# Casting loads in batch 0 for seven GpSimd casts, and VectorE's list of batch 0 in another order

## The chip, the cores and the metric

The kernel runs on one core of a Trainium2 chip. Time is device microseconds of that core for one execution, the median of several runs; lower is better. Five engines run lists of their own and wait for each other through semaphores: TensorE (PE, matmuls, with weight loads as PEld beside them), VectorE (DVE), ScalarE (ACT), GpSimd (POOL) and SyncE (SP). DMAs are issued from SP's and POOL's lists. A list is run strictly in order: an instruction that waits holds everything behind it on its engine.

## The reference

Two parts in a row, for eight batches of S = 3072 tokens with D = 256, a query width of 64 and a hidden width of 1024:

```python
scores = (1.0 / S) * np.matmul(z, z.transpose(0, 2, 1))
attn = np.maximum(scores, 0.0) ** 2
x = u * np.matmul(attn, v)
h1 = x @ w1
h2 = x @ w2
g = np.maximum(h1, h2)
out = g @ w_out
```

All inputs and the output are float32; the kernel computes in bfloat16 with float32 sums.

## The kernel before

**Scores.** `z` is laid out transposed in `zT`. A batch's scores are cut into 6 x 6 blocks of 512 x 512. Scores are symmetric, so only the upper triangle is computed: `score_pair` (L248) makes half a block, that is two tiles of 128 keys by 512 queries. Two matmuls go to PSUM (`s_ps`, L267), a ReLU copies them out (L277 in one piece, L284 in two halves on ACT; L282 is a half on VectorE for pairs called "shared"), and `finish()` squares them: L294 on VectorE in one operation of 1024 columns, L290 in halves, L292 on ACT. The lower blocks are made by a transposing DMA on SP's queue (`mirror`, L315). A block lives in one of 27 homes (`Block`, taken from the list `free`); `mirror_ready` issues a mirror only while more than one home is free.

**Batch 0, groups 0 to 3** (`PLAIN` = 4, the loop from L946). A group is 512 queries. `attn_unit` (L331) multiplies 24 key tiles by both halves of `v`, two 64-row matmuls per step. Between the steps, at slots given by hand, the loop emits score pairs (at most 11 ahead of what PE needs), and at chosen tile numbers `n` all the other work: the group's sums (`drain_fast`, L355 and L356, then L982), the product with `u` (`gate`, L499), the transposes of `u` (`turn_u`, L243), loads and casts.

**Loads and casts.** `load_u` and `load_v` are DMAs from POOL's queue that cast float32 to bfloat16 on the way (L235, L209). `staged` (L164) instead loads float32 from SP's queue into a `Block`; `load_staged` (L172) and `z_staged` (L178) then cast on POOL. The homes used for staging rest in a list until `rested` gives them back. At the start, tokens 12 to 23 of `z` are loaded as float32 from POOL's queue and cast by POOL (L147).

**Weights.** max(h1, h2) is computed as ReLU(x(w1 - w2)) + x w2, and the second term needs only `W2o` = w2 w_out. So `w15` = w1 - w2 is made on VectorE (L1022), w2 is transposed on PE (L1027) and copied out (L1028), and `W2o` is a matmul of that with `w_out` (L1035).

**The first feed-forward parts.** Groups go in couples. `second(i, tasks)` runs the feed-forward of a couple and puts a list of tasks, nearly all on VectorE, ahead of it in program order: for the first two couples `ff` (L746 inner, L768 outer products, L759 ReLU), later `ff_by_seven`, which uses a seven-product form of the matrix product with four weight forms `wT_sb` (`weight_forms`, L531 to L536).

**Groups 4 and up, couple by couple** (L1239). Attention too uses seven products instead of eight, with combinations of `v` (`combine_v`, four operations per piece, L223 to L226) and of score blocks (`prepare` and `combine`, L369). Some combinations are made early, in the list ahead of the feed-forward before; others late, between the steps. A combination S3 of batch 1 is written over a block that a mirror's DMA still reads. Batch 0's last couple mixes both ways (`MIXED_LANES`). Sums leave PSUM through `kept` (L1137, a copy) and `add` (L1133).

**The order of the tasks.** `prepared(i)` returns v's combinations and the early forms, per piece of `v`: four v operations, then two forms. Just before the first `ff`, `first` is the number of tasks put ahead of it.

The lines that the change touches are the two that hold the order of gates and of weight forms,

```python
                if i and n in (12, 15):
                    tasks[n // 15]()
```

```python
            second(i - 1, tasks, **({} if b else {"order": (2, 3, 0, 1)}))
            if not b:
                for do in weight_forms():
                    do()
```

and the ones in the diff below.

Of the kernel before, what the change touches and what calls it, by code (L numbers as in the profile page):

```python
# [12 lines left out]
def kernel(  # L13
# [10 lines left out]
    nc = tc.nc  # L24
# [15 lines left out]
    NC = NG // 2  # L40
# [36 lines left out]
    def by_tile(x):  # L77
        return x.rearrange("(p t) d -> p t d", t=NT)
# [151 lines left out]

    un, uT = {}, {}

    def load_u(b, g):
        un[b, g] = unat.tile([P, G, D], bf16, name="un")
        nc.gpsimd.dma_start(out=un[b, g], in_=by_tile(u[b])[:, ds(g * G, G), :])  # L235

    def u_staged(b, g):
# [609 lines left out]
    def emit_pair(wait=0, shared=False, act=False, late=False):  # L847
        nonlocal done
        shared = shared or done < 12 and done % 3 == 0
        finish = score_pair(  # L850
            *pairs[done], dve_half=1 if shared else None, halves=done == 0, act=act
        )
        done += 1
        if late:
            late_squares.append(finish)
        elif wait:
            due.append((tick + wait, finish))
        else:
            finish()
# [33 lines left out]
    with tc.manual_schedule():  # L893
# [4 lines left out]
        nc.vector.memset(warm[:, P:], 0.0)  # L898
        load_v(0, 0, 0, G)
        make_identity(nc, ident)  # L900
        z32.update({lo: first_z(lo, n, nc.gpsimd) for lo, n in ((12, 8), (20, 4))})
        load_v(0, 0, G, G)
        for piece in range(1, NC):
            for lo in (0, G):
                load_v(0, piece, lo, G)
        load_u(0, 0)
        load_u(0, 1)
        z_first.append(Block())
        for pad in (-1, NT):
            nc.vector.memset(z_bf16(pad, 1), 0.0)  # L910
        w2, w2T = Block(), Block()
# [23 lines left out]
        keep_warm([P] * 5)  # L935
        cast_z(nc.scalar.copy, z32[5], 5, 3)
        cast_z(nc.vector.tensor_copy, z32[5], 8, 4, at=3)
        for at in range(0, 8, 4):
            cast_z(nc.gpsimd.tensor_copy, z32[12], 12 + at, 4, at=at)
        cast_z(nc.gpsimd.tensor_copy, z32[20], 20, 4)  # L940
        emit_pair()
        zT_pe(5, 7, [(nc.scalar.copy, 3), (nc.vector.tensor_copy, 4)])
        keep_warm([P] * 2)
# [5 lines left out]
        for i in range(PLAIN):  # L949
            b, g = groups[i]  # L950
            if i:
                acc = new_acc()
            if i == 3:
                rested(len(resting) - 1)
            new, slots = {}, pair_slots(i)
            for slot, (n, dc) in enumerate(steps_of(i)):
                k = need(b, g, n)
                upto = max(k, min(done + 1, k + AHEAD)) if slot in slots else k
                while done < min(upto, len(pairs)):
                    emit_pair(  # L960
                        wait=int(i < 2 and slot == slots[-1]), shared=i == 3 and done % 3 == 1
                    )
                if i == 0 and slot in (8, 22):
                    if slot == 8:
                        zT_pe(12, 8, [(nc.scalar.copy, 4)] * 2)
                    else:
                        zT_pe(20, 5, [(nc.scalar.copy, 5)])
                    if slot == 22:
                        for x in z_first:
                            x.release()  # L970
                attn_unit(b, g, n, acc, dc, n == 0, n == NT - 1)
                if n == NT - 1 and i < PLAIN - 1:
                    if i < 2:
                        new[dc] = drain_fast(acc, dc)
                        flush()
                    else:
                        new.update(drain(acc, [dc]))
                if dc:
                    continue
                if i in (1, 2) and n in (6, 9):  # L980
                    h = sums[n // 9]
                    nc.vector.tensor_add(h[0], h[0], h[1])  # L982
                    sums[n // 9] = h[0]
                if i and n == 12:
                    xTs[groups[i - 1]], tasks = gate(*groups[i - 1], sums)
                if i and n in (12, 15):
                    tasks[n // 15]()
                if i == 0 and n == 14:
                    turn_u(0, 0)
                if (i, n) == (0, 16):  # L990
                    turn_u(0, 1)
                if (i, n) == (0, 20):
                    nc.vector.memset(w2_sb[:, 0, 0:1], 0.0)
                    nc.gpsimd.dma_start(out=w2_sb, in_=by_chunk(moe_w2))
                if (i, n) == (1, 9):
                    w1_32 = [staged(w2_sb[:, c : c + 1], by_chunk(moe_w1)[:, c : c + 1]) for c in range(KD)]
                if (i, n) == (1, 11):
                    u_staged(0, 2)
                if (i, n) == (1, 13):
                    for h in range(2):  # L1000
                        part = slice(h * KF // 2, (h + 1) * KF // 2)
                        load_staged(w_out_sb[:, part], by_chunk(moe_w_out)[:, part])
                if (i, n) in ((1, 15), (2, 14), (3, 4)):
                    z_staged(1, i - 1)
                if (i, n) == (2, 2):
                    turn_u(0, 2)
                if (i, n) == (2, 5):
                    u_staged(0, 3)
                if (i, n) == (2, 17):
                    turn_u(0, 3)  # L1010
                if (i, n) in ((2, 18), (3, 1)):
                    u_staged(0, 4 + (i > 2))
                if (i, n) in ((2, 10), (3, 10)):
                    turn_z(1, i - 2)
                if (i, n) == (3, 16):
                    turn_z(1, 2)
                if later and n % 4 == 0 and (i == 3 or i and n > 12):
                    later.sort(key=lambda block: (block[2] > 3, block[1], block[2]))
                    mirror(*later.pop(0))
                if i == 2 and n == 16:  # L1020
                    for c in range(KD):
                        nc.vector.tensor_sub(w15_sb[:, c : c + 1], w1_32[c], w2_sb[:, c : c + 1])  # L1022
                if i == 2 and n in (15, 18):
                    half = n // 18
                    tp = mm_tile([P, KF, P], bf16, "tpw")[0]
                    for j in range(KF):
                        nc.tensor.transpose(tp[:, j, :], w2_sb[:, half, ts(j, P)], ident)  # L1027
                    nc.scalar.copy(w2T_sb[:, half, :, :], tp)  # L1028
                if i == 2 and n == 18:
                    w2.release()  # L1030
            if i == 2:
                for dc in range(KD):
                    ps = mm_tile([P, D], fp32, "w2o_ps")[0]
                    for nb in range(KF):
                        nc.tensor.matmul(  # L1035
                            ps,
                            w2T_sb[:, dc, nb, :],
                            w_out_sb[:, nb, :],
                            start=(nb == 0),
                            stop=(nb == KF - 1),  # L1040
                        )
                    nc.scalar.copy(W2o_sb[:, dc, :], ps)
                w2T.release()
            sums = new
# [25 lines left out]
        def prepared(i):  # L1070

            b, c = couples[i]
            for o in range(NC):
                assert all(
                    pair_at[b, min(q, k), 2 * max(q, k) + 1] < done
                    for q in (2 * c, 2 * c + 1)
                    for k in (2 * o, 2 * o + 1)
                ), (i, done)
            forms, early, late = prepare(b, c)
            split = {}  # L1080
            for n, o in enumerate(forms):
                if (b, o) not in vt:
                    split[n] = combine_v(b, o)
            if not b:
                return forms, [do for dos in split.values() for do in dos] + early, [], late
            last_v = split.pop(NC - 1, []) if b > 1 else []
            early = [
                do for n in range(NC) for do in split.get(n, []) + early[2 * n : 2 * n + 2]
            ]
            return forms, early, last_v, late  # L1090

        b, g = groups[PLAIN - 1]
# [5 lines left out]
        loads_behind(PLAIN // 2 - 1)  # L1098
        forms, early, last_v, late = prepared(PLAIN // 2)
        first = 4 * NC + len(forms)  # L1100
        second(PLAIN // 2 - 2, sums + early[:first])
        xTs[b, g], gates = gate(b, g, {dc: h[0] for dc, h in halves.items()})
        for do in gates + early[first:]:
            do()
# [2 lines left out]
        for i in range(PLAIN // 2, len(couples)):  # L1107
# [10 lines left out]
            n_pairs = target - done  # L1118
            at_step = {}
            for n in range(n_pairs):  # L1120
                at_step.setdefault(2 + n * (len(steps) - 2) // max(n_pairs, 1), []).append(n)
            acc, opened, h = {}, {}, {}
            left = {}
            if not b:
# [9 lines left out]

            def kept(name, of):
                h[name] = new_h()
                nc.scalar.copy(h[name], acc[of])  # L1137

            def after_p5():
                add(h["V"], h["V"], acc["P5"])  # L1140
# [144 lines left out]
                ]  # L1285
            mm_pool("mm_single")
            second(i - 1, tasks, **({} if b else {"order": (2, 3, 0, 1)}))
            if not b:
                for do in weight_forms():
                    do()  # L1290
            if at_last:
                for do in token_forms(b, c):
                    do()
# [38 lines left out]
```

## Time and profile before

| | |
|---|---|
| median of 3 runs | 890.31 us (889.68 to 890.57) |
| the profiled execution: its own time | 890.65 us |
| its span, first to last instruction | 888.7 us |
| granted TensorE clock | 1.00 |
| PE busy | 879.2 us, 99% |
| VectorE busy | 796.7 us, 90% |
| ACT busy | 723.2 us, 81% |
| POOL busy | 100.6 us, 11% |

Times inside a profile count from the span's start. Groups 0 to 3 of batch 0 run from about 6 to 63 us, the first feed-forward from 63 to 79, batch 0's last couple from 79 to 103, the second feed-forward from 103 to 119, and batch 1's first couple from 119 to 141. By stage (busy us of each engine):

| window us | PE | VectorE | ACT | POOL |
|---|---|---|---|---|
| 20 to 36 | 15.85 | 12.05 | 14.22 | 0.43 |
| 36 to 43 | 7.00 | 6.30 | 6.54 | 6.46 |
| 62 to 80 | 17.89 | 11.69 | 12.24 | 3.43 |
| 104 to 119 | 14.95 | 10.80 | 10.17 | 0.00 |
| 119 to 136 | 16.48 | 16.90 | 14.42 | 2.12 |

In a line of the order of time, the columns are start, duration, engine, line, operation, the tile written and those read, shapes and count; the bracket tells how long the engine had been idle before and what ended that. A line of waits has the total in us, the number of times and the longest.

### The profile page before, as it was taken

The page shows a single profiled execution, that of the slowest core. Times are in us where ns is not written, and L with a number is a line of the kernel's source. Part 1 is how long each engine was busy: PE and PEld are TensorE (multiplying, and loading weights), DVE is VectorE, ACT ScalarE, POOL GpSimd, SP SyncE. Part 2 cuts the span into 40 slices and gives each one's busy share as a digit, 9 for nine tenths or more (in the row PEclk, how much of TensorE's full clock was granted, in tenths as well). Part 3 has the DMA queues.
Part 4 walks back from the last instruction along what each step waited for, and adds up shares of the span by engine and source line. Part 5 has one row for each costly group of instructions (what it writes and reads, how often), then busy time and mean ns, then how long its engine had stood idle before and what let it go on. Part 6 is the DMA issues. An engine that isn't in the chain of part 4 may idle for free.

```text
span 888.7 us, 19366 instructions
## 1 busy us (share of the span) xinstructions
PE 879.2 (99%) x7395; PEld 505.8 (57%) x7443; DVE 796.7 (90%) x1256; ACT 723.2 (81%) x1144; POOL 100.6 (11%) x176
## 2 busy tenths in 40 slices
PE   9999999999999999999999999999999999999997
PEld 4555656565565555655646556566465564655655
DVE  6897789999998999989999899998999988998965
ACT  7987887889888888888888888888888889884544
POOL 3222100111102011020111101011100110000000
PEclk9999999999999999999999999999999999999999
DMA  9999999989999899997999989999999989897302
GB/s 179 250 224 191 195 208 152 202 124 199 176 173 178 168 174 165 202 167 159 149 171 190 163 167 180 153 199 135 196 163 150 187 132 200 153 148 161 84 1 96
DMA packets 396013, 148.09 MB, mean 167 GB/s; under 512 B 361264, under 2 KB 375856, under 8 KB 395920
## 3 DMA queue, kind: packets, MB, share of 16 engines
q1 hardware_dynamic: 373488, 119.32, 74.2%
q0 software_dynamic: 22288, 27.40, 23.7%
q8 instruction: 58, 0.95, 0.5%
q14 instruction: 35, 0.29, 0.1%
q10 hardware_dynamic: 144, 0.13, 0.0%
HBM read 59.77 MB, written 25.17 MB: 96 GB/s over the span
## 4 chain that ended last, share of the span: by engine, by line
PE 95%; DVE 3%; issue 1%; DMA 1%; ACT 0%; DVEq 0%
PE acc L1239 44%; PE acc L579 22%; PE d_ps L640 13%; PE s_ps L267 7%; PE acc L331 4%; PE acc L768 1%; PE d_ps L602 1%; PE d_ps L746 1%; DVE blk L369 1%; DMA blk<-blk 1%; DVE blk L294 1%; PE acc L927 0%; DVE xT L499 0%; DVE h_sb L982 0%; DVE blk L290 0%
## 5 line engine op out<-in xcount | busy, mean ns | idle before, releaser
L1239 PE MATMUL acc<-blk,v_sb 64*128 64x512 bf16 x2144 | 387.6, 376 | 0.5 <-DVE h_sb L1133 0.4
L369 DVE TENSOR_TENSOR blk<-blk,blk 128x2048 bf16<-128x2048 bf16 x260 | 312.5, 1218 | 16.2 <-DMA blk<-blk 10.0
L1239 PE MATMUL acc<-blk,vt 64*128 64x512 bf16 x1560 | 317.0, 376 | 0.0
L277 ACT ACTIVATE blk<-s_ps 128x1024 bf16<-128x1024 f32 x212 | 214.3, 1021 | 32.0 <-PE s_ps L267 30.2
L1239 PEld LDWEIGHTS <-v_sb 64*128 64x128 bf16 x2144 | 152.8, 94 | 125.0 <-issue 5.0
L579 PE MATMUL acc<-w_out_sb,g_sb 128*128 128x256 bf16 x1344 | 182.5, 273 | 0.8
L1239 PEld LDWEIGHTS <-vt 64*128 64x128 bf16 x1560 | 124.1, 94 | 75.6 <-issue 1.5
L579 PEld LDWEIGHTS <-g_sb 128*128 128x128 bf16 x1344 | 131.5, 98 | 53.0
L652 DVE CUSTOM_DVE_ANT_0 g_sb<-blk,d_ps 128x512 bf16<-128x512 f32 x187 | 123.1, 684 | 21.6 <-ACT blk L648 14.7
L267 PE MATMUL s_ps<-zT 64*128 64x512 bf16 (+3 forms) x672 | 126.5, 357 | 0.6 <-DVE zT L155 0.3
L648 ACT COPY blk<-d_ps 128x512 f32<-128x512 f32 x193 | 111.3, 590 | 16.8 <-PE d_ps L640 13.4
L615 ACT ACTIVATE g_sb<-d_ps 128x512 bf16<-128x512 f32 x149 | 86.7, 599 | 18.6 <-PE d_ps L640 15.3
L294 DVE TENSOR_TENSOR blk<-blk 128x1024 bf16<-128x1024 bf16 x129 | 86.0, 684 | 13.0 <-ACT blk L277 12.9
L292 ACT ACTIVATE blk<-blk 128x1024 bf16<-128x1024 bf16 x83 | 87.6, 1056 | 1.2
L640 PE MATMUL d_ps<-blk,wT_sb 128*128 128x512 bf16 x242 | 87.3, 379 | 0.0
L284 ACT ACTIVATE blk<-s_ps 128x512 bf16<-128x512 f32 (+3 forms) x160 | 61.2, 437 | 24.8 <-PE s_ps L267 24.5
L209 POOL DMA_DIRECT2D v_sb<-in_v_dram x90 | 48.4, 554 | 260.2 <-PE acc L1239 209.7
L1133 DVE TENSOR_TENSOR h_sb<-h_sb,acc 128x512 f32<-128x512 f32 x89 | 58.7, 682 | 14.5 <-PE acc L1239 13.7
L499 DVE SCALAR_TENSOR_TENSOR xT<-h_sb,uT 128x512 bf16<-128x512 f32 x96 | 61.3, 688 | 0.7 <-DMA uT<-un 0.7
L267 PEld LDWEIGHTS <-zT 64*128 64x128 bf16 x672 | 36.2, 94 | 37.4 <-DVE zT L155 0.5
L684 ACT COPY o_sb<-acc 128x512 f32<-128x512 f32 x86 | 48.3, 590 | 8.6 <-PE acc L579 6.3
L1137 ACT COPY h_sb<-acc 128x512 f32<-128x512 f32 x66 | 38.6, 584 | 19.5 <-PE acc L1239 17.8
(96 smaller groups left out, 800.9 us busy)
## 6 DMA issues: line engine op xcount, KB each, us to landing
out_dram<-o_sb SPq DMA_DIRECT2D x95, 256.0 KB, 3.3
un<-in_u_dram POOLq DMA_DIRECT2D x44, 256.0 KB, 5.6
v_sb<-in_v_dram POOLq DMA_DIRECT2D x84, 128.0 KB, 6.7
blk<-blk SPq DMA_TRANSPOSE x240, 5.2
zn<-in_z_dram POOLq DMA_DIRECT2D x18, 128.0 KB, 4.9
blk<-in_u_dram SPq DMA_DIRECT2D x4, 512.0 KB, 4.5
v_sb<-in_v_dram POOLq DMA_DIRECT2D x6, 256.0 KB, 5.8
blk<-in_moe_w_dram SPq DMA_DIRECT2D x2, 512.0 KB, 4.7
```

What stands on the lines that cost most here:

```text
L267: nc.tensor.matmul(s_ps[h][:, lo[h] :], zT[rows, z_at(b, blk * G + tiles[h], h), :], zT[rows, q + lo[h] // P : q + G, :].rearrange("p t c ...
L277: nc.scalar.activation(r, two, AF.Relu)
L292: nc.scalar.activation(both, r, AF.Square)
L294: nc.vector.tensor_mul(both, r, r)
L369: op(*((by_key(x) if mixed else x.ap) for x in blocks))
L499: lambda dc=dc: nc.vector.scalar_tensor_tensor(out=x[:, dc, :].rearrange("p (t r) -> p t r", r=P), in0=hs[dc].rearrange("p (t r) -> p t r" ...
L579: nc.tensor.matmul(o_ps[key][:, t % 2, :], x[:, ts(t, P)], w, start=first, stop=not left[key] and t % 2 == 1, skip_group_check=last,)
L615: nc.scalar.activation(g, ps, AF.Relu)
L640: nc.tensor.matmul(ps, w, x, start=first, stop=ends, skip_group_check=True)
L648: nc.scalar.copy(u_[k, name], ps)
L652: nc.vector._custom_dve(TENSOR_ADD_SAT, out=g, in0=u_[k, with_], in1=ps, s0=float("inf"), s1=0.0)
L1239: mm = nc.tensor.matmul(a.out(acc[name]), w()[rows], a.moving(rows, j), start=first, stop=left[name] == 0, skip_group_check=True,)
```

## The change

It replaces POOL's casts of `z` 12 to 23 (three), of `u` of groups 2 and 3 and of `w_out` (two) by DMAs that cast on the way, issued from POOL. For `u` and `w_out` a small memset on VectorE goes first, which the DMA has to wait for, so that it doesn't start sooner than that place in VectorE's list:

```diff
-    def load_u(b, g):
+    def load_u(b, g, held=False):
         un[b, g] = unat.tile([P, G, D], bf16, name="un")
+        if held:
+            nc.vector.memset(un[b, g][:, 0, 0:1], 0.0)
         nc.gpsimd.dma_start(out=un[b, g], in_=by_tile(u[b])[:, ds(g * G, G), :])
...
-        z32.update({lo: first_z(lo, n, nc.gpsimd) for lo, n in ((12, 8), (20, 4))})
+        z_first.append(Block())
+        for lo, n in ((12, 8), (20, 4)):
+            nc.gpsimd.dma_start(
+                out=z_bf16(lo, n).rearrange("p (t d) -> p t d", d=dqk),
+                in_=by_tile(z[0])[:, ds(lo, n), :],
+            )
...
-        for at in range(0, 8, 4):
-            cast_z(nc.gpsimd.tensor_copy, z32[12], 12 + at, 4, at=at)
-        cast_z(nc.gpsimd.tensor_copy, z32[20], 20, 4)
...
                 if (i, n) == (1, 11):
-                    u_staged(0, 2)
+                    load_u(0, 2, held=True)
                 if (i, n) == (1, 13):
-                    for h in range(2):
-                        part = slice(h * KF // 2, (h + 1) * KF // 2)
-                        load_staged(w_out_sb[:, part], by_chunk(moe_w_out)[:, part])
+                    nc.vector.memset(w_out_sb[:, 0, 0:1], 0.0)
+                    nc.gpsimd.dma_start(out=w_out_sb, in_=by_chunk(moe_w_out))
...
                 if (i, n) == (2, 5):
-                    u_staged(0, 3)
+                    load_u(0, 3, held=True)
```

In groups 1 to 3, the square of pair 21 (the last pair of group 1) is done in halves; the second gate operation of group 1 moves from tile 15 to 16 of group 2, both of group 2 move from tiles 12 and 15 to 14 and 17 of group 3; the first of the two copies of the transposed w2 goes from ACT to VectorE; and the subtractions that make `w15` move from tile 16 to 18:

```diff
-            *pairs[done], dve_half=1 if shared else None, halves=done == 0, act=act
+            *pairs[done], dve_half=1 if shared else None, halves=done in (0, 21), act=act
...
-                if i and n in (12, 15):
-                    tasks[n // 15]()
+                if i and n in (12 if i < 3 else 14, (0, 15, 16, 17)[i]):
+                    tasks[n > 14]()
...
-                if i == 2 and n == 16:
-                    for c in range(KD):
-                        nc.vector.tensor_sub(w15_sb[:, c : c + 1], w1_32[c], w2_sb[:, c : c + 1])
...
-                    nc.scalar.copy(w2T_sb[:, half, :, :], tp)
+                    (nc.scalar.copy if half else nc.vector.tensor_copy)(w2T_sb[:, half, :, :], tp)
                 if i == 2 and n == 18:
+                    for c in range(KD):
+                        nc.vector.tensor_sub(w15_sb[:, c : c + 1], w1_32[c], w2_sb[:, c : c + 1])
                     w2.release()
```

Behind the groups, for batch 1's first couple each form comes one place later among the operations that combine `v`; the weight forms move from behind the second feed-forward's tasks to among the first one's; in batch 0's last couple the score pairs are spread over four steps less, and the copy of the sum U2 goes from ACT to VectorE:

```diff
             last_v = split.pop(NC - 1, []) if b > 1 else []
+            ahead = int(b == 1)
             early = [
-                do for n in range(NC) for do in split.get(n, []) + early[2 * n : 2 * n + 2]
-            ]
+                do
+                for n in range(NC)
+                for do in split.get(n, []) + early[max(2 * n - ahead, 0) : 2 * n + 2 - ahead]
+            ] + early[2 * NC - ahead :]
...
-        second(PLAIN // 2 - 2, sums + early[:first])
+        second(PLAIN // 2 - 2, sums + early[: first - 4] + weight_forms() + early[first - 4 : first])
...
-                at_step.setdefault(2 + n * (len(steps) - 2) // max(n_pairs, 1), []).append(n)
+                at_step.setdefault(2 + n * (len(steps) - (2 if b else 6)) // max(n_pairs, 1), []).append(n)
...
             def kept(name, of):
                 h[name] = new_h()
-                nc.scalar.copy(h[name], acc[of])
+                copy = nc.vector.tensor_copy if not b and name == "U2" else nc.scalar.copy
+                copy(h[name], acc[of])
...
             second(i - 1, tasks, **({} if b else {"order": (2, 3, 0, 1)}))
-            if not b:
-                for do in weight_forms():
-                    do()
```

More of the change, by code (lines that the diff above doesn't have):

```diff
@@ L907 @@
         load_u(0, 1)
-        z_first.append(Block())
         for pad in (-1, NT):
```

## The prediction

> **What bounds the kernel now.** I read the page's busy line, then the waits of PE, then the order of time of PE and of whichever engine PE waited for.
>
> ```profile
> PE 879.2 (99%) x7395; PEld 505.8 (57%) x7443; DVE 796.7 (90%) x1256; ACT 723.2 (81%) x1144; POOL 100.6 (11%) x176
> ```
>
> PE is the bound; only its holes can be won. The waits of PE name few:
>
> ```profile
> PE acc L1239 <- DVE h_sb L1133: 0.4, 1, 0.4
> PE s_ps L267 <- DVE r_sb L282: 0.3, 1, 0.3
> PE acc L331 <- DVE blk L294: 0.2, 1, 0.2
> ```
>
> The ends of matmuls are modelled, so shorter holes hide in long runs. Two 64-row matmuls of 512 columns share a step; two L267 lines with eight L331 between them lie 1.08 us apart, five steps, so a step is 0.216 us. I compare starts with that:
>
> ```profile
> 7.51 1.13 PE L331 MATMUL acc<-blk,v_sb 64*128 64x512 bf16 x6
> 31.52 0.83 PE L331 MATMUL acc<-blk,v_sb 64*128 64x512 bf16 x6
> 32.50 2.19 PE L331 MATMUL acc<-blk,v_sb 64*128 64x512 bf16 x18 [0.15 <-DVE blk L294]
> 43.08 1.06 PE L331 MATMUL acc<-blk,v_sb 64*128 64x512 bf16 x6
> 60.51 1.03 PE L331 MATMUL acc<-blk,v_sb 64*128 64x512 bf16 x7
> 97.50 0.93 PE L1239 MATMUL acc<-blk,v_sb 64*128 64x512 bf16 x4
> 133.25 0.37 PE L1239 MATMUL acc<-blk,v_sb 64*128 64x512 bf16 x1 [0.43 <-DVE h_sb L1133]
> ```
>
> Six matmuls take 0.83 us where nothing is late: the run at 43.08 loses 0.23, that at 7.51 up to 0.30. After 31.52 the fourth step was due at 32.17 and came at 32.50: 0.33. A score pair is followed by L331 after 0.21 us; the pair at 59.83 got it at 60.51: 0.47. Four half-steps at 97.50 should take 0.70: 0.23. At 132.45 the next step came 0.59 late, and two more behind it 0.27 and 0.06 late: 0.92. From 141 us on each couple repeats its pattern and no wait is named. The holes in reach sum to about 2.4 us, all where VectorE is late.
>
> ```profile
> 37.24 2.38 DVE L294 TENSOR_TENSOR blk<-r_sb 128x1024 bf16<-128x1024 bf16 x2 [0.51 <-ACT r_sb L284]
> 39.54 1.52 DVE L982 TENSOR_TENSOR h_sb<-h_sb 128x512 f32<-128x512 f32 x1
> 40.98 1.09 DVE L294 TENSOR_TENSOR blk<-r_sb 128x1024 bf16<-128x1024 bf16 x1
> 42.00 1.09 DVE L982 TENSOR_TENSOR h_sb<-h_sb 128x512 f32<-128x512 f32 x1
> 58.73 1.12 DVE L499 SCALAR_TENSOR_TENSOR xT<-h_sb,uT 128x512 bf16<-128x512 f32 x1
> 77.67 1.22 DVE L369 TENSOR_TENSOR blk<-blk,blk 128x2048 bf16<-128x2048 bf16 x1 [5.08 <-DMA blk<-blk]
> 116.11 1.23 DVE L369 TENSOR_TENSOR blk<-blk,blk 128x2048 bf16<-128x2048 bf16 x1 [2.58 <-DMA blk<-blk]
> 117.25 0.42 DVE L223 TENSOR_TENSOR vt<-v_sb 128x512 bf16<-128x512 bf16 x1
> 121.24 0.42 DVE L531 TENSOR_TENSOR wT_sb<-w_sb 128x512 bf16<-128x512 bf16 x1
> 123.09 2.49 DVE L499 SCALAR_TENSOR_TENSOR xT<-h_sb,uT 128x512 bf16<-128x512 f32 x4
> ```
>
> ```profile
> 36.09 1.55 POOL L172 CAST un<-blk 128x1024 bf16<-128x1024 f32 x1 [15.65 <-DMA blk<-in_u_dram]
> 37.58 2.94 POOL L172 CAST w_out_sb<-blk 128x1024 bf16<-128x1024 f32 x2
> ```
>
> **Casts into loads.** Gone from POOL: three z casts (1.92 us from 7.48), u of group 2 (1.55), w_out (2.94), u of group 3 (1.96 at 48.52). While POOL casts, VectorE is slow: between 20 and 34 us an L294 has a median of 0.68, from 37.24 on 0.93, 1.30 and 1.09; L982 takes 1.52 and 1.09 for 0.68. Excess 2.5 us. The square at 43.01, ready at 43.69, is what PE waited for at 43.74: 0.23 won. At 7.11 an L294 took 0.87, and PE started with its end: 0.18 won of that hole. The zd casts stay; the first (2.08 us) comes earlier, before squares that had 1.03 and 0.51 us of idle ahead, and costs by the same ratio 0.8 us there: nothing on PE.
>
> The Trainium skill, "SBUF — State Buffer", section "Who interferes with whom", says VectorE with two SBUF inputs and a GpSimd operation that reads SBUF exclude each other on a shared port; the stretched L294 agree.
>
> New are four load issues on POOL (0.53 to 0.71 us, rows of L235 and L994; POOL idles) and three VectorE memsets: 0.06 us each (L993), between 0 and 0.11 (L897's 128x64). Two fall between 28 and 30 us, where the square of pair 20 ends at 31.6 and is due at 31.7. I charge 0.07 (0 to 0.2). Each memset waits for its buffer: that of u of group 2 for the transpose of u of group 0, issued at 19.32 and landed 7.7 later, at 27.04; VectorE gets there at about 28.1. Behind it stand squares 18 to 21, which PE takes 0.1 to 0.4 us after they are made: cover 1.1 us, after that every microsecond is PE's. Group 3's buffer is free at 29.3, its memset due near 38. On POOL's queue w_out stands behind u of group 2 and ahead of the zd casts; w2, the same size, took 6.4 us to land, so w_out lands near 38 and is due at 48.25 (L1035). u of group 3 stands behind the zd cast; its gate is at 83. SP sheds four issues (2.1 us), and the staging blocks they held are free for mirrors. z lands as before (6.7 to 7.0), due at 9.22.
>
> **Square of pair 21 in halves.** The first half needs only the first ReLU and ends before 32.17, the second is due a step later: 0.33 won (0.1 if both slide). Two L290 of 512 step 0.34 each for 0.61: 0.07, with idle behind.
>
> **Gates of group 2 later in group 3.** L282, whose bank PE waits for, stands behind the gate L499 (1.04 step) at 58.73. Now it goes first and ends near 59.4, due at 59.83: 0.47 won. Gates of groups 0 and 1 hardly move.
>
> **Copies.** The first w2 transpose goes from ACT (1.01) to VectorE: L155 took 0.42 for 512 and 0.49 for 640 columns, so about 0.70 for 1024; at most 1.36, two L356. It pays from the 2.5 us above; PE wants the bank at 44.85, some 0.6 us after. Cover gone, up to 0.7. w15's two subtractions (2.34) move two tiles later, first read at 63.6: nothing. U2's copy ran on ACT at 97.21 behind an L277 of 1.02 and PE resumed at 97.84 with its end; VectorE stood idle 0.60 before 97.35, and L356, the same form, takes 0.69 from 96.8: 0.23 won. Pairs spread over 82 instead of 86 steps: nothing, at most 0.1 either way.
>
> **Weight forms and v's combinations.** The four forms (121.24 to 123.09, 1.85 us) move into the first feed-forward's list, ahead of the form that waits 5.08 us for a transpose: free. The last four v operations (1.59) go ahead of the one that waits 2.58 us until 116.02. So the gates at 123.09 start 3.44 earlier. PE arrives about 1.4 earlier, ACT with it; VectorE is 2.0 better off, where 0.92 was missing: 0.92 won.
>
> **Sum.** 0.18 + 0.33 + 0.23 + 0.47 + 0.23 + 0.92 - 0.07 = 2.3 us. Span 888.7 to 886.4; with the 1.95 around it (890.65 that execution) 888.35; that execution lies 0.34 over the median of 890.31, so **888.0**.
>
> **Rivals.**
>
> *The transposes hold VectorE at 116 us.* They land one after another on SP's queue to 126 us; if the one of 116.02 slides as PE comes earlier, the 0.92 stays: 888.9. For: that wait is on a landing. Against: it must slide 1 us or more, and SP has less ahead. Chance 0.11.
>
> *Casting loads starve a transpose.* Between 21.5 and 25.5 us the software queue moved 0.50 MB and the hardware queue 0.10 MB, though that did 0.90 MB between 17 and 21 alone. u of group 2 and w_out write 0.75 MB: 6 us at that rate, from about 30.4. The mirror that group 2 reads first needs the engines from 29.0 to 30.6; caught, it lands near 37.0, due at 35.6: 1.4 lost, 889.4. Against: it is mostly through by then. Chance 0.09.
>
> The Trainium skill, "DMA: Bandwidth & Descriptors", section "Queues, rings and completion order", has the engines take turns between queues packet by packet, which those two shares fit.
>
> *Slower: the memset stops VectorE.* If its wait counts a later landing on SP's queue (29.3, the mirror's 31.6, w1's 33.4) instead of 27.04, VectorE stands until then with PE behind it: with the mirror's 3.5 us, 891.5, with w1's 5.3 us, 893.3. It makes the whole slower from a landing after 30.4. For: VectorE runs its list in order, and the squares behind it have no cover of their own. Against: before, the cast into that buffer had the same condition. Chance 0.08, half of it beyond 892.1.
>
> *The holes move.* PE comes earlier, and the same squares and ReLUs are late elsewhere (ACT 0.89 busy between 20 and 36): 890.3. Chance 0.07.
>
> **From this to the numbers.** The forecast has 0.65 with its own range of 887.3 to 888.7. A measurement tells 0.2%, 1.8 us, from no change: faster means under 888.5. Faster 0.63 (nearly all of the forecast's, and a bit of the first rival), same 0.30, slower 0.07. The range is 887.3 to 890.0: below lies only what all bounds together give, above the slow rival and part of the last.
>
> **What would show it.** PE's waits on L282 and L1133 gone; steps at 43, 60 and 97 even; squares at 0.68 between 36 and 43; the gates of 123.09 near 118 (PE's gain in); no idle of VectorE before the memset near 28. A memset with idle before it, an L331 waiting on a transpose near 36, or a hole near 133 makes it wrong.

## The result, and the profile after

The changed kernel took 894.71 us (median of 20 runs, 888.85 to 898.92) and the kernel before, beside it, 890.45 us (20 runs, 889.62 to 894.49): a ratio of 1.0036 with a 95% interval of 1.0022 to 1.0049. It is 0.4% slower, and 4.7 us above the end of the range that was forecast. The profiled execution took 894.71 us with a span of 892.9 us, where that of before had 888.7.

The busy line of the changed kernel shows that PE's work is the same and that POOL lost its casts (line numbers in its profile are shifted by a few against those of before: L333 is L331 there, L296 is L294, L1244 is L1239):

```profile
PE 879.7 (99%) x7395; PEld 506.3 (57%) x7443; DVE 797.2 (89%) x1262; ACT 722.0 (81%) x1142; POOL 94.7 (11%) x172
```

The holes that the change aimed at in groups 0 to 3 are gone or smaller. These are the runs of matmuls of the changed kernel that answer to those at 7.51, 32.50 and 60.51 (PE in order of time: start, length, line, operands):

```profile
7.61 1.00 PE L333 MATMUL acc<-blk,v_sb 64*128 64x512 bf16 x6
...
31.50 2.12 PE L333 MATMUL acc<-blk,v_sb 64*128 64x512 bf16 x18
...
58.57 0.40 PE L269 MATMUL s_ps<-zT 64*128 64x512 bf16 x2
58.79 1.04 PE L333 MATMUL acc<-blk,v_sb 64*128 64x512 bf16 x8
59.65 0.40 PE L269 MATMUL s_ps<-zT 64*128 64x512 bf16 x2
```

The six at 7.61 take 1.00 us for 1.13 (0.83 where nothing is late). From 31.50 all run through without a break, where before the seventh (the fourth step) came 0.33 late, and around 59 us the score pairs stand 1.08 apart, five steps, with nothing missing. VectorE between 35 and 41 us has short squares, and the last of the three memsets stops nothing:

```profile
35.69 0.69 DVE L296 TENSOR_TENSOR blk<-r_sb 128x1024 bf16<-128x1024 bf16 x1 [1.03 <-ACT r_sb L286]
36.89 0.69 DVE L296 TENSOR_TENSOR blk<-r_sb 128x1024 bf16<-128x1024 bf16 x1 [0.51 <-ACT r_sb L286]
37.54 0.06 DVE L236 MEMSET un<- 128x1 bf16 x1
37.97 0.69 DVE L296 TENSOR_TENSOR blk<-r_sb 128x1024 bf16<-128x1024 bf16 x1 [0.38 <-ACT r_sb L286]
38.58 1.10 DVE L985 TENSOR_TENSOR h_sb<-h_sb 128x512 f32<-128x512 f32 x1
```

But PE's waits name others, all longer than those that the prediction lists (line, what it waited for, us in total, times, longest):

```profile
PE s_ps L269 <- DMA zT<-zd: 1.7, 1, 1.7
PE acc L333 <- DMA blk<-blk: 1.4, 1, 1.4
PE acc L1244 <- DVE h_sb L1137: 1.3, 1, 1.3
PE acc L1244 <- POOLq L1253: 1.0, 1, 1.0
```

In PE's order of time they stand at four places (a mirror's block, a transposed z, a sum, and a no-op in POOL's list):

```profile
53.40 1.04 PE L333 MATMUL acc<-blk,v_sb 64*128 64x512 bf16 x8 [1.38 <-DMA blk<-blk]
...
92.93 0.39 PE L269 MATMUL s_ps<-zT 64*128 64x512 bf16 x2 [1.71 <-DMA zT<-zd]
...
96.10 0.80 PE L1244 MATMUL acc<-blk,v_sb 64*128 64x512 bf16 x5 [1.27 <-DVE h_sb L1137]
...
164.04 0.39 PE L1244 MATMUL acc<-blk,v_sb 64*128 64x512 bf16 x1 [1.01 <-POOLq L1253]
```

Counted in steps as in the prediction (a matmul's start against the end of the step ahead of it), PE lost 1.56, 1.87, 1.54 and 1.28 us there, 6.25 in all. All gaps of 0.25 us or more sum to 2.96 us before and 7.23 after: 4.3 more, against a span that grew by 4.2. So the whole difference between the two profiled executions is in these gaps; about 2 us were won and 6.25 lost.

The first of the four is a mirror, group 3's first (L317). It was issued at 44.09 and landed 9.3 us later, at 53.35. In the kernel before it was issued at 44.70 and landed 5.6 later, at 50.31, 2 us ahead of its reader. The answers on that one instruction, of the changed kernel and then of the kernel before, end with:

```profile
L317 SPq DMA_TRANSPOSE blk<-blk x1: 7192/7192/7192, 44.1 to 44.1; - x1
...
  PE acc L333: 1.4, 1
...
DMA to landing us min/median/max: 9.3/9.3/9.3
```

```profile
L315 SPq DMA_TRANSPOSE blk<-blk x1: 3576/3576/3576, 44.7 to 44.7; - x1
...
DMA to landing us min/median/max: 5.6/5.6/5.6
```

The DMA queues between 43 and 50 us (packets, MB, share of 16 engines; the hardware queue carries what SP issues, the software queue POOL's loads) show what else ran; a share adds up packets that overlap and can pass 100%. First after, then before:

```profile
DMA packets 1680, 0.67 MB, mean 95 GB/s; under 512 B 1551, under 2 KB 1551, under 8 KB 1679
...
q1 hardware_dynamic: 1537, 0.39, 85.4%
q0 software_dynamic: 142, 0.26, 50.1%
```

```profile
DMA packets 5048, 1.76 MB, mean 252 GB/s; under 512 B 4919, under 2 KB 4919, under 8 KB 5047
...
q1 hardware_dynamic: 5047, 1.76, 120.6%
```

Both queues are busy, and together they move 95 GB/s where the hardware queue alone moved 252. What is on the software queue is the casting load of u of group 3: POOL issued it at 39.08, and it took 11.4 us. When it was issued w_out's casting load (30.11, landed 40.83) was still under way. POOL's list:

```profile
30.11 0.89 POOL L1004 DMA_DIRECT2D w_out_sb<-in_moe_w_out_dram  x1 [0.88 <-DVE w_out_sb L1003]
37.02 2.11 POOL L178 CAST zd<-blk 128x512 bf16<-128x512 f32 x2 [6.02 <-DMA blk<-in_z_dram]
39.08 0.54 POOL L237 DMA_DIRECT2D un<-in_u_dram  x1
```

The other three gaps stand behind late transposes further down SP's queue. zT at 93 us landed at 92.89 for 86.92 before. The one at 164 comes by way of POOL's list: PE waits there for a no-op that POOL runs as a relay between two matmuls (L1253), and ahead of it a load of u stood until the transpose that still read its buffer had landed, at 163.34. In the chain (start, length, what):

```profile
160.10 3.24 DMA uT<-un
...
163.36 0.04 POOLq L237
163.40 0.47 issue
163.88 0.02 POOLq L1253
...
164.04 0.45 PE acc L1244 x2
```

And two early forms (L371, combinations of score blocks), which waited for transposes until 77.7 and 79.8 before, came 3 us later:

```profile
80.67 1.23 DVE L371 TENSOR_TENSOR blk<-blk,blk 128x2048 bf16<-128x2048 bf16 x1 [4.18 <-DMA blk<-blk]
83.06 3.50 DVE L371 TENSOR_TENSOR blk<-blk,blk 128x2048 bf16<-128x2048 bf16 x3 [1.16 <-DMA blk<-blk]
86.47 1.29 DVE L501 SCALAR_TENSOR_TENSOR xT<-h_sb,uT 128x512 bf16<-128x512 f32 x2
...
95.36 1.28 DVE L1137 TENSOR_TENSOR h_sb<-h_sb,acc 128x512 f32<-128x512 f32 x2
```

VectorE runs its list in order. It stood idle 4.18 and 1.16 us and then had forms, gates and squares in a heap; the sum h_sb that PE waits for at 96.10 is behind them.

### The profile page after: what moved, and what is told of

Read it like the earlier page. It is cut to its first block, busy times and chain, and to the rows that moved or that the text cites. A ratio compares the mean times of both kernels' runs of the same rounds, so it can differ in the third digit from the quotient of the medians.

```text
span 892.9 us, 19359 instructions
## 1 busy us (share of the span) xinstructions
PE 879.7 (99%) x7395; PEld 506.3 (57%) x7443; DVE 797.2 (89%) x1262; ACT 722.0 (81%) x1142; POOL 94.7 (11%) x172
## 4 chain that ended last, share of the span: by engine, by line
PE 94%; DMA 3%; DVE 2%; issue 1%; ACT 0%; SPq 0%; POOL 0%; POOLq 0%; DVEq 0%
PE acc L1244 43%; PE acc L581 21%; PE d_ps L642 13%; PE s_ps L269 7%; PE acc L333 4%; PE acc L770 2%; PE d_ps L748 2%; DMA blk<-blk 2%; PE d_ps L604 1%; DMA uT<-un 1%; DVE blk L371 1%; DVE blk L296 1%; PE acc L933 0%; PE tpz L152 0%; PE acc L712 0%
## 5 line engine op out<-in xcount | busy, mean ns | idle before, releaser
L1244 PE MATMUL acc<-blk,v_sb 64*128 64x512 bf16 x2144 | 387.9, 376 | 2.4 <-DVE h_sb L1137 1.3
L371 DVE TENSOR_TENSOR blk<-blk,blk 128x2048 bf16<-128x2048 bf16 x260 | 313.1, 1221 | 14.4 <-DMA blk<-blk 10.2
L1244 PE MATMUL acc<-blk,vt 64*128 64x512 bf16 x1560 | 317.3, 376 | 0.0
L1244 PEld LDWEIGHTS <-v_sb 64*128 64x128 bf16 x2144 | 152.4, 94 | 127.9 <-issue 6.4
L1244 PEld LDWEIGHTS <-vt 64*128 64x128 bf16 x1560 | 124.0, 94 | 75.3 <-issue 0.9
L269 PE MATMUL s_ps<-zT 64*128 64x512 bf16 (+3 forms) x672 | 130.4, 357 | 1.8 <-DMA zT<-zd 1.7
L296 DVE TENSOR_TENSOR blk<-blk 128x1024 bf16<-128x1024 bf16 x129 | 86.3, 688 | 11.3 <-ACT blk L279 11.2
L294 ACT ACTIVATE blk<-blk 128x1024 bf16<-128x1024 bf16 x83 | 87.6, 1056 | 1.2
L1137 DVE TENSOR_TENSOR h_sb<-h_sb,acc 128x512 f32<-128x512 f32 x89 | 58.9, 684 | 14.4 <-PE acc L1244 13.6
L237 POOL DMA_DIRECT2D un<-in_u_dram x46 | 24.4, 531 | 298.1 <-DMA uT<-un 103.4
```

Of the source, the lines that this page charges most:

```text
L269: nc.tensor.matmul(s_ps[h][:, lo[h] :], zT[rows, z_at(b, blk * G + tiles[h], h), :], zT[rows, q + lo[h] // P : q + G, :].rearrange("p t c ...
L294: nc.scalar.activation(both, r, AF.Square)
L296: nc.vector.tensor_mul(both, r, r)
L371: op(*((by_key(x) if mixed else x.ap) for x in blocks))
L1244: mm = nc.tensor.matmul(a.out(acc[name]), w()[rows], a.moving(rows, j), start=first, stop=left[name] == 0, skip_group_check=True,)
```

## The experiments

Three theories were tested: that casting loads hold up SP's transposes, and which of the three does; that the holes only moved because PE came earlier; and, from the first four runs on, that the cost is that of two casting loads under way together. Each kernel ran beside the kernel before on the same chip: its medians were 890.95 (first four), 890.76 (next four) and 891.01 us (last three).

| kernel | median us | ratio, 95% interval | span | w_out landed | load of u of group 3: issued, took | PE's gaps |
|---|---|---|---|---|---|---|
| e1, three loads staged again | 892.17 | 1.001 (0.9992–1.0028) | 890.2 | – | – | 4.85 |
| e2, w_out staged | 890.6 | 0.9993 (0.9979–1.0008) | 889.1 | – | 43.36, 4.4 | 3.79 |
| e3, u of group 3 staged | 896.33 | 1.0057 (1.0036–1.0078) | 894.8 | 41.29 | – | 8.22 |
| e4, before + three casting loads | 891.18 | 1.0006 (0.9982–1.0031) | 888.5 | 41.80 | 40.65, 8.2 | 3.15 |
| e5, e2 + w2T's copy on ACT | 892.9 | 1.0023 (1.0006–1.0039) | 889.5 | – | 42.66, 4.4 | 4.04 |
| e6, w_out in long rows | 890.21 | 0.9997 (0.9987–1.0006) | 887.6 | 39.63 | 41.29, 5.2 | 2.31 |
| e7, u of group 3 staged apart | 889.53 | 0.9996 (0.998–1.0012) | 887.5 | 41.30 | – | 2.31 |
| e8, changed kernel, one execution | 897.93 | – | 896.2 | 40.89 | 39.30, 10.8 | 7.60 |
| e9, u of group 3 seven tiles later | 888.9 | 0.9977 (0.9961–0.9993) | 886.2 | 41.05 | 43.17, 4.8 | 1.32 |
| e10, e9 + w_out in long rows | 890.97 | 1.0002 (0.9982–1.0022) | 893.0 | 39.49 | 43.69, 5.4 | 6.30 |
| e11, changed kernel again | 893.25 | 1.0022 (1.0007–1.0037) | 894.8 | 41.45 | 39.53, 11.0 | 8.09 |

(Span, landings and gaps are those of the one profiled execution, which need not be the median one: e9's was the fastest of its twelve, e10's the second slowest, e11's the slowest. Gaps of 0.25 us or more, summed over the span; "–" where there is no such load or no interval.)

**e1, e2, e3: the casting loads taken back.** e1 puts staging and POOL casts back for u of group 2, w_out and u of group 3; e2 does the second hunk alone, e3 the third alone:

```diff
-                    load_u(0, 2, held=True)
+                    u_staged(0, 2)
...
-                    nc.vector.memset(w_out_sb[:, 0, 0:1], 0.0)
-                    nc.gpsimd.dma_start(out=w_out_sb, in_=by_chunk(moe_w_out))
+                    for h in range(2):
+                        part = slice(h * KF // 2, (h + 1) * KF // 2)
+                        load_staged(w_out_sb[:, part], by_chunk(moe_w_out)[:, part])
...
-                    load_u(0, 3, held=True)
+                    u_staged(0, 3)
```

> The changed kernel with u of groups 2 and 3 and w_out loaded as float32 from SP's queue and cast by POOL again; the casting loads of z and all of VectorE's new order stay. Theory A (the casting loads starve the transposes of SP's queue, and every new hole of PE hangs on a late transpose): the holes of 1.6, 1.9, 1.5 and 1.3 us at 53, 93, 96 and 164 us go, the order's gains stay but for POOL's casts beside VectorE (0.4): about 888.5 us, and the runs lie within 2 us of each other. Theory B (PE merely comes earlier and meets the same transposes): two or more of the holes stay, 891 to 895.

> The changed kernel with w_out alone staged and cast by POOL again. Theory A with w_out's 512-byte packets as the main cost (it ran from 34.5 to 40.3 us with the transposes at a quarter of their rate): most of the loss goes, 889 to 890. Theory A with u of group 3 as the main cost (its 256 KB took from 43 to 50 us): little goes, 893 to 894. Theory B: unchanged, 894 to 895.

> The changed kernel with u of group 3 alone staged and cast by POOL again. Theory A with u of group 3 as the main cost: the hole at 53 us goes and the later ones shrink, 889 to 890, with a spread of some 2 us. With w_out as the main cost: 893 to 894. Theory B: unchanged, 894 to 895.

In e1 and e2 the gaps at 53, 93 and 164 us are gone: the casting loads are their cause, not PE's lead. The one near 95, on the h_sb sum, is down to 1.11 and 0.62, but it does not go: e6 (0.79), e7 (1.62) and e10 (1.29), where no slow load of u of group 3 is about, have it too. There the early forms waited for their transposes until 77.1 to 77.6 and 79.5 to 80.0, about as in the kernel before; that PE comes sooner to a sum behind the same transposes fits, but was not tried. Neither e1 nor e2 won anything, for a new wait took the place (PE's waits in e2):

```profile
PE s_ps L269 <- DVE blk L1028: 1.1, 1, 1.1
PE acc L933 <- DVE blk L899: 1.0, 1, 1.0
PE acc L1245 <- DVE h_sb L1138: 0.4, 1, 0.4
```

L1028 (L1027 in the changed kernel) is the copy of the first half of w2T, which the change moved to VectorE. With w_out's casts back on POOL, VectorE's squares beside them take 1.05 and 1.52 us again, the copy is late behind them, and PE loses 1.32 us at 46.4 (in e1 the same at 47.2, and 0.82 at 44.8). e3 lost 7.01 us at one place, and not on PE's own transposes. Of VectorE's waits in e3:

```profile
DVE blk L296 <- DMA blk<-blk: 8.2, 1, 8.2
```

A square waited until 60.77 for a block to write into that a mirror, issued at 55.88, was still reading. That the staging block of u, taken from the same list of free blocks, gives every later square another block is tested in e7.

**e4: the loads alone.** The kernel before with the three loads and memsets of the change (the first and third hunk of e1 and the second, the other way round), and nothing else of it.

> The kernel before with the three casting loads of u and w_out and their memsets, and nothing else of the change. Theory A: the transposes slip by some 3 us as in the changed kernel; PE comes some 1.5 us later to them and keeps the holes that late VectorE work made, so 892 to 896, with a wide spread. Theory B (what hurts is that PE comes earlier): within 1 us of the kernel before, 889.5 to 891.

No difference from before can be told (its twelve executions lie between 888.76 and 900.47 us): the mirror (issued 44.86) took 6.7 us and landed at 51.59, 1.3 us later than before, within its 2 us of cover. So the load of u of group 3 is slow there too (8.2 us), but it was issued with 1.15 us of w_out's time to go, for 1.75 in the changed kernel, and less came of it. By its median alone e4 lies nearer to what was expected if PE's coming earlier made the loss (889.5 to 891) than to what the loads were to cost (892 to 896); e9, where PE comes as early as in the changed kernel, decides against the first.

**e5: the copy back on ACT.** To see whether e2's new wait was all that it lacked:

```diff
-                    (nc.scalar.copy if half else nc.vector.tensor_copy)(w2T_sb[:, half, :, :], tp)
+                    nc.scalar.copy(w2T_sb[:, half, :, :], tp)
```

> The run with w_out alone staged, and in addition the first copy of the transposed w2 back on ACT. If the hole of 1.3 us at 46 us in that run comes from the copy standing behind squares that POOL's casts stretch, it goes: 889.3 (890.6 - 1.3), holes of 0.3 and 0.6 us left at 58 and 94. If VectorE is late there whatever it carries, the hole stays under another name: 890.6.

The expectation of 889.3 us was missed. The gap at 46 is gone, but one of 3.27 us came at 59.5, behind another square (L296) that waited 4.13 us for a block that a mirror was reading (landed 58.09): e3's wait in small. Staged loads draw on the blocks of the squares, and each way of staging runs into another of their transposes.

**e6: fewer packets for w_out.** In the changed kernel w_out goes in 512-byte packets. Here each partition gets rows that lie side by side in DRAM. They then stand in another order than the hidden units, so the output is made with the wrong rows of w_out; the kernel leaves out putting them back in order:

```diff
-                    nc.gpsimd.dma_start(out=w_out_sb, in_=by_chunk(moe_w_out))
+                    nc.gpsimd.dma_start(out=w_out_sb, in_=moe_w_out.rearrange("(p c) f -> p c f", c=KF))
```

> The changed kernel, with w_out loaded by the same casting DMA but row p*8+c at place c of partition p, so that a partition's 8 KB lie in one piece; its rows then stand in another order than the hidden units, so the second term of the output and g @ w_out use wrong rows. If the packets of 512 bytes are what starves the transposes for 6 us, packets of 2 KB and more take some 3.3 us, the transposes come 2 to 3 us sooner, and the time is 890 to 892. If any casting load of that size does it: 894 to 895.

Its median is 890.21 us, where the changed kernel had 894.71 and, in e11, 893.25. w_out landed at 39.63 and u of group 3 was issued at 41.29, only 2.2 us later than in the changed kernel, but behind w_out's end (the zd cast ahead of it in POOL's list waited for z until 39.69, for 37.02); it took 5.2 us for 11.4, and the mirror landed at 49.15. Whether the packets or the order did it is left to e10.

**e7: u of group 3 staged in a block of its own.** As e3, but its staging block is one that no square uses until batch 1:

```diff
+    spare = apool.tile([P, G * GW], bf16, name="spare")
...
+        if (b, g) == (0, 3):
+            t = spare.bitcast(fp32)[:, : G * D].rearrange("p (a f) -> p a f", a=G)
+            nc.sync.dma_start(out=t, in_=by_tile(u[b])[:, ds(g * G, G), :])
+            nc.gpsimd.tensor_copy(un[b, g], t)
+            return
...
-                    load_u(0, 3, held=True)
+                    u_staged(0, 3)
```

> The changed kernel with u of group 3 staged and cast by POOL, in a home that no score block uses before batch 1 (its 28th), so that no other block's home shifts. If the 7 us hole of the earlier run with u of group 3 staged came from a square waiting for a home that a mirror still read, it is gone; then u of group 3's casting load costs what this run gains on the changed kernel: theory 'both loads' 891 to 892, theory 'w_out' 893 to 894. If the hole stays, staging u of group 3 itself makes it: 896.

e3's gap is gone, so it came from the blocks. And with w_out still a casting load (30.42 to 41.30) beside SP's transposes, nothing is late at 53: w_out's load by itself is covered. The largest gap that is left, 1.62 us at 93, is the h_sb sum.

**e8 and e11: the changed kernel again**, unedited.

> The changed kernel once more, for a second profile. Theory A: the landings of w_out and of u of group 3 differ from the first profile's 40.8 and 50.5 us, and the time and the holes near 53, 93, 96 and 164 us follow the transposes that stand behind them: with landings 3 us sooner, 889 to 891, with the same, 894 to 896. Were the spread elsewhere, the landings would be the same within 0.5 us and the time not.

> The changed kernel unchanged, timed beside these on the same chip: 893 to 896 median with a spread of 5 us or more, if the loss is the kernel's own; under 891 if the earlier runs' chip made it.

In both, u of group 3 was issued while w_out was under way and took 10.8 and 11.0 us, and PE lost 7.6 and 8.1 us. The places differ (52.8, 85.4, 96.2 and 148.4 in e8; 53.4, 93.2, 96.2 and 165.2 in e11): what is fixed is the late transposes, and which of their readers has the least margin varies.

**e9: the load of u of group 3 seven tiles later.** One line of the changed kernel:

```diff
-                if (i, n) == (2, 5):
+                if (i, n) == (2, 12):
                     load_u(0, 3, held=True)
```

> The changed kernel with the casting load of u of group 3 (and its memset) seven tiles later in group 2, at tile 12 instead of 5, so that POOL issues it near 42.7 us, after w_out has landed (40.8 to 41.3) instead of before. Theory C (what costs is two casting loads in flight at once: issued at 39.1 behind an unfinished w_out, u of group 3 took until 50.5 and kept the transposes at a fifth of their rate; issued after w_out's landing, it took 4.4 and 5.2 us in two runs): it lands near 48, the holes at 53 and 164 go, 889 to 890.5. Theory 'any casting load there': it lands 7 us or more after its packets begin and the time is 893 to 895.

It is faster than both kernels: 888.9 us against 891.01 of the kernel before (ratio 0.9977, 0.9961 to 0.9993) and 893.25 of the changed one (e11) beside it on the same chip. The span of the profiled execution, the fastest of twelve, is 886.2. PE's waits, the whole list:

```profile
PE acc L933 <- DVE blk L899: 1.0, 1, 1.0
PE d_ps L642 <- issue: 0.2, 1, 0.2
```

None of the four is left. The load and the queues between 43 and 50 us:

```profile
L237 POOL DMA_DIRECT2D un<-in_u_dram x1: 540/540/540, 43.2 to 43.2; - x1
...
DMA to landing us min/median/max: 4.8/4.8/4.8
```

```profile
DMA packets 4562, 1.37 MB, mean 196 GB/s; under 512 B 4434, under 2 KB 4434, under 8 KB 4562
...
q1 hardware_dynamic: 4418, 1.11, 77.9%
q0 software_dynamic: 144, 0.26, 22.9%
```

The same 0.26 MB goes over the software queue in the same stretch, beside the same transposes, but needs less than half of the engines' time, and the hardware queue moves 1.11 MB for 0.39. w_out landed at 41.05, ahead of this load's issue.

**e10: e9 with w_out in long rows**, the line of e6 added, to part packets from order.

> The same with u of group 3 later, and w_out loaded in long rows as in the earlier run (rows in another order than the hidden units, so the second term and g @ w_out use wrong rows). If w_out's 512-byte packets cost time of their own once u of group 3 is out of their way: 0.5 to 1.5 us under the run with u of group 3 later alone. If w_out's load is covered as it stands: the same within 0.5 us.

The long rows won nothing on top of e9, so w_out's small packets cost nothing that can be told once u of group 3 comes behind them, and e6's gain fits the order. Long rows with both loads under way together were not run. The profiled execution had a bad stretch of its own further on, where two casting loads of u (18.1 us from issue to landing, median of the two) and transposes meet. VectorE, which waits for z there:

```profile
142.97 0.50 DVE L192 COPY zd<-zn 128x512 bf16<-128x512 bf16 x2 [4.75 <-DMA zn<-in_z_dram]
...
143.98 1.88 DVE L1137 TENSOR_TENSOR h_sb<-h_sb,acc 128x512 f32<-128x512 f32 x3
```

PE lost 3.50 us at 144.72 behind that h_sb. A mirror issued at 125.72 took until 146.21; in e9 the same one, issued at 123.69, landed at 134.54. These loads are in the kernel before as well. That such stretches come in some executions and not in others would be enough for the spread of its runs (888.93 to 895.06 beside e10), but this was not tried.

## Why the prediction was wrong

- **PE's holes and their sizes** were right. e9, which is the changed kernel but for one load, has a median 2.1 us below the kernel beside it where 2.3 were summed. That its profiled span is 886.2 where 886.4 was forecast is partly luck, since that execution is the fastest of twelve; its median is 888.9 for the 888.0 of the forecast. The waits on L282 and on the sum L1133 (now L284 and L1137) are gone there, and the gaps fell from 2.96 to 1.32 us.
- **Shorter squares** were right: 0.69 us at 35.7, 36.9 and 38.0. They are 1.05 and 1.52 again in e2 with the casts back, which bears out how the prediction read POOL's casts.
- **The copy of w2T** was sized right (0.70 forecast, 0.68 measured). Its cover was under-sized: "up to 0.7" with the cover gone, 1.32 us lost in e2 and in e1.
- **The memsets** stop nothing (0.06 us at 28.31, 29.74 and 37.54, no wait named): the slower rival did not happen.
- **The step that failed** is the costing of the loads: "w_out lands near 38 and is due at 48.25", "u of group 3 stands behind the zd cast; its gate is at 83", "SP sheds four issues". Each load was held against its own reader, and SP's queue was credited with what it loses. Both loads are in time (40.83, 50.50) and cost nothing that way. What u's load costs is paid by the transposes that run while it does, and their readers stand on PE's path: 3 us of lateness at the mirror, of which PE sees 1.56 at 53 us, and 4.69 more at 93, 96 and 164. Not all of the 4.69 is u's: the 1.54 at 96 holds a wait on h_sb that e6, e7 and e10 have without it.
- **The rival "casting loads starve a transpose"** had the mechanism, from the row at 21.5 to 25.5 us. It took it for u of group 2 and w_out at group 2's mirror, with 1.4 us; there nothing waited. The same row had to be held against every casting load that meets transposes: u of group 3 has 0.25 MB, half of what the row shows, and the mirror it meets had 2 us to spare.
- **The rivals of moved holes and of the transposes at 116 us** do not show in e9, whose trace has one gap between 10 and 850 us, 0.36 at 91.67. But the wait on h_sb there, 0.62 to 1.62 us in e1, e2, e6, e7 and e10, is a hole that the kernel before does not have, of the kind that the rival of moved holes expects. e4, which has the loads without the new order, shows 0.54 of it, so how much of it belongs to PE's lead is open.

Shown: the loss belongs to the load of u of group 3 and its place (e9 beside e11, and e7). That being under way together with w_out is what matters fits all nine executions with a casting load of u of group 3: it took 8.2 to 11.4 us when it was issued ahead of w_out's end (changed kernel, e4, e8, e11), 4.8 to 5.4 behind it (e6, e9, e10), and 4.4 where w_out was no casting load (e2, e5). It is not shown apart from the time of issue: the four slow ones were issued at 39.08 to 40.65, the five others at 41.29 to 43.69. A load issued at 39 with w_out out of the way was not run. Open: why the slow stretch lasts until 50 us when w_out has landed at 41.

## What to carry to other kernels

A load that is moved to another queue is costed twice: once against its own reader, and once against everything that the shared DMA engines carry while it runs, with the margin of each transfer's reader written beside it. Here loads that cast in flight did best one after another, issued behind the landing of the one ahead where their reader can wait; seven tiles of delay were worth 4 us. When staged loads and results share one pool of blocks, a load added or taken away changes which transfer each later result must wait for (7 us in e3).

## What the runs showed of the hardware

In the slow stretch the median packet is as quick as ever; a minority hold the engines. Packets that started between 43 and 50 us, of one size on each queue:

| kernel | queue, bytes | packets | median ns | over 250 ns | us in those | us in all | longest us |
|---|---|---|---|---|---|---|---|
| before | hardware, 256 | 4807 | 18 | 35 | 21.4 | 110.1 | 0.71 |
| after | hardware, 256 | 1509 | 18 | 79 | 35.8 | 91.0 | 1.44 |
| after | software, 2048 | 128 | 173 | 52 | 42.7 | 56.0 | 2.04 |
| e9 | hardware, 256 | 4322 | 18 | 10 | 5.0 | 86.0 | 1.40 |
| e9 | software, 2048 | 128 | 173 | 14 | 5.5 | 25.3 | 0.72 |

The long packets end in heaps. From 41 us on, in the changed kernel, 22 end together at 42.6 us and smaller heaps follow until 50.3; e9 has such heaps too, but fewer, the largest with 21 at 44.4. A busy share of the DMA engines therefore says little of what they move: 85.4% and 50.1% stood for 95 GB/s, 77.9% and 22.9% for 196.

A long hole can cost PE more than its own length. In four places of these traces the granted TensorE clock is 0.50 for 3.41 us, beginning 0.1 to 1.2 us after PE resumed from a hole of 2.15 us or more (e8 behind 96.15 and 148.43, e10 behind 144.72, e11 behind 165.18), and in e3 it is 0.50 for 6.83 us from 60.39, a point inside its hole of 7.01. A step then takes 0.43 us for 0.216. The row of e11 (stretch; busy us of PE, PEld, VectorE, ACT and POOL; clock; DMA):

```profile
165.80:169.10 3.30, 3.30 (x20) 1.65 (x17) 2.96 (x7) 1.18 (x4) 1.28 (x3) 0.50 1.22 190
```

Span less gaps is 885.7 us in the profiled executions of both kernels, where no hole ahead of the end did this, and 888.6 in e8, 886.7 in e11. Length alone does not decide it: the hole of 3.27 us in e5 left the clock at 1.00.

The Trainium skill, "DMA: Bandwidth & Descriptors", section "Issuing engines are not separate DMA queues", says that DMAs of all issuing engines run on the same 16 engines and interleave, and that issuing on several saves only the time to issue. The trace agrees with the first, since the transposes of one queue are late through a load of the other. No run here tests the second alone, since the cast and the queue change with the issuing engine; what counted was which transfers ran together: u of group 3 as a casting load from POOL made the kernel 894.71 and 893.25 us, as a plain load from SP with a cast behind it 889.53 (e7), and 888.9 from POOL again but later (e9).
